# The z sums of a linear-attention layer on VectorE, and its FFN weights and transposes placed anew

## The chip, the cores and the metric

The kernel runs on one core of a Trainium2 chip. The core has TensorE (PE, matmuls into PSUM), VectorE (DVE), ScalarE (ACT), GpSimd (POOL) and SyncE (SP), which here only issues DMAs. The metric is the device time of one execution in microseconds. The kernel before takes 817.4 us, the median of 5 runs from 817.06 to 817.52.

## The reference

One transformer block, forward and backward, in bf16: x has 2048 tokens of D = 640, with H = 32 heads of 20, and the FFN is 1728 wide. Only the part in which the change lies is shown.

```python
def _A_ref(x, wqkv, wo):                      # x is layernormed
    ...
    phi = lambda t: jnp.where(t > 0, t + 1, jnp.exp(t)) + 1e-6
    pq, pk = phi(q), phi(k)
    kv = jnp.einsum("bhsd,bhse->bhde", pk, v)
    z = jnp.einsum("bhsd->bhd", pk)
    num = jnp.einsum("bhqd,bhde->bhqe", pq, kv)
    den = jnp.einsum("bhqd,bhd->bhq", pq, z)[..., None] + 1e-6
    o = num / den
    return ... @ wo
h = x + _A_ref(_layernorm(x), A_wqkv, A_wo)
h2 = h + _B_ref(_layernorm(h), ...)           # (silu(x @ w_gate) * (x @ w_up)) @ w_down
```

The kernel gives h2 and the gradients of x and of all weights for a given grad_out. z, one number per column of pk, is the sum of pk over all 2048 tokens.

## The kernel before, in words

Tokens lie in 16 tiles of 128 (partitions), columns in 5 blocks of 128; a row of 640 columns goes through PSUM as two halves of 320. All of PSUM is four buffers of two banks (`mm`, line 63), given out in turn. SBUF has two pools of large buffers, `big` (5 tiles with tag B) and `strips` (4 with tag S); a new tile waits until the last reader of the one whose place it takes has ended, a DMA among them.

The stages around the change, with the times of the profiled execution:

1. **Layernorm, q and k** (lines 324 to 383, until 55 us). `kq_mm` makes k and q of a tile; ACT writes exp and relu of them; `phi` (line 310) makes pk and pqa of that on DVE with two instructions, and every four tiles stores pk, or pq and xnT, on SP. The last calls, for the tiles 12 to 15, are at lines 374 to 376.
2. **Y and z** (lines 478 to 494, 55 to 86 us). Y^T = xn^T pk in five columns of 2 x 16 matmuls (line 482). `z_sum` (line 467) sums pk over the tokens with 32 matmuls against ones of 128 x 32, of which four use different 32-column strips of PE; ACT and DVE split the sum into a bf16 value and a bf16 remainder; four matmuls with 1/32 (line 489) sum the partitions, giving zb, the same in every partition, by which DVE gets the denominators.
3. **Normalise** (`normalise`, line 439, four tiles at a time): product with zb, sum over each head, reciprocal, multiply into pqa, and then `tr_pqs` (line 450), one DMA transpose per tile into pqsT. Groups 0 and 4 come after Y, groups 8 and 12 after W2.
4. **KVT and W2** (lines 501 to 524, 86 to 95 us): small matmuls, masked on DVE, then W2^T with one DMA transpose per block.
5. **The attention loop** (lines 533 to 565, 98 to 146 us). Per tile, ten matmuls (`ps_a`, line 539), the residual added on DVE into the x row `xr`, statistics on DVE, rstd on POOL. Two iterations later the row goes out to `scr_h1` from ACT's queue, `hn` is written on DVE, and SP transposes it into hnT. `load_xr` loads the x rows ahead, into six small buffers.
6. **FFN** (from line 568, 146 us). Four weight groups. pg and pu (lines 593 and 598) need `hnT` and the gate and up weights of the group, `wgu`, loaded by `load_wgu` (line 182) into one of two buffers; group 0 takes that of wdT, which the dm steps of groups 0 and 1 read.

**dm steps** (`dm_steps`, line 399): 24 pieces of ten matmuls of 448 or 384 columns for the backward pass, which need nothing of the attention. They are put between other work by `dm(n)`: nine ahead of the attention loop, one inside its first row and one after each of the rows 1 to 14.

**The order of the work.** Inside `tc.manual_schedule(engines=...)` the named engines issue in the order of the program; the others are ordered by a planner that estimates costs. From line 461 on that is so for PE, DVE and SP, so ACT and POOL are planned. A DMA stands in the queue of the engine that issues it. `tc.keep_in_program_order` fixes one instruction, `tc.issue_after(x)` puts what follows behind x on x's engine.

Of the kernel before, what the change touches and what calls it, by code (L numbers as in the profile page):

```python
# [20 lines left out]
def kernel(  # L21
# [159 lines left out]

    def load_wgu(g):
        w = GW[g]
        t = wpool.tile([P, DT, 2 * GM], BF16, name="wgu", tag="wgu")
        nc.sync.dma_start(out=t[:, :, 0:w], in_=B_w_gate[:, GO[g]:GO[g] + w].rearrange("(k p) n -> p k n", p=P))
        nc.sync.dma_start(out=t[:, :, w:2 * w], in_=B_w_up[:, GO[g]:GO[g] + w].rearrange("(k p) n -> p k n", p=P))
        return t

# [41 lines left out]
    with tc.manual_schedule(engines={EngineType.Pool}):  # L230
# [6 lines left out]
        E = const.tile([P, D], BF16, name="E")  # L237
    ones32 = const.tile([P, P], BF16, name="ones32")
    nc.vector.memset(ones32[:], 1.0 / H)
    zpad = const.tile([P, 4, 64], BF16, name="zpad")  # L240
# [69 lines left out]
    def phi(which, t, n=2):  # L310
        e = (pk, pqa)[which][:, t:t + n, :]
        nc.vector.tensor_scalar(out=e, in0=e, scalar1=1.0, scalar2=1e-6, op0=ALU.min, op1=ALU.add)
        nc.vector.tensor_tensor(out=e, in0=e, in1=rr[:, 2 * which + t // 2 % 2, t % 2:t % 2 + n, :], op=ALU.add)
        if (t + n) % 4 == 0:
            sl = slice(t + n - 4, t + n)
            if which == 0:
                nc.sync.dma_start(out=scr_pk_v[:, sl, :], in_=pk[:, sl, :])
            else:
                nc.sync.dma_start(out=scr_pq_v[:, sl, :], in_=pqa[:, sl, :])
                nc.sync.dma_start(out=scr_xnT[sl].rearrange("t p k c -> p t k c"), in_=xnT[:, sl])  # L320

    PIECES = ((0, 3), (3, DT))

    with tc.manual_schedule(engines={EngineType.PE, EngineType.DVE, EngineType.Activation, EngineType.Pool}):
# [33 lines left out]
        for t in range(2, ST):  # L358
            if t == 2:
                ln1_stats(4)  # L360
            if t > 3 and t + 3 < ST:
                ln1_stats(t + 3)
            kq_mm(t, 0, (lambda: copy1(t + 1)) if t + 1 < ST else None)
            if t == 2:
                ln1_stats(5)
            if t == 3:
                ln1_stats(6)
            if t == ST - 1:
                phi(0, t - 1, 1)
            kq_mm(t, 1)  # L370
            if t == 3:
                phi(1, 0)
            elif t == ST - 1:
                phi(0, t, 1)
                phi(1, t - 3)
                phi(1, t - 1)
            elif t > 3:
                phi(t % 2, t - 2 - t % 2)
            if t + 2 < ST:
                ln1_xn(t + 2)  # L380
            if ST - NC - 1 <= t < ST - 1:
                ln1_xn(t - ST + NC + 1)

    fA.close()
    fpool = wB.enter_context(tc.tile_pool(name="fpool", bufs=6))

# [32 lines left out]
    def masks():  # L421
        tc.keep_in_program_order(nc.gpsimd.memset(mask[:], 1.0))
        for c0, n, p0 in ((0, 6, 0), (120, 2, 88)):
            m = mask[:, c0:c0 + n * Dh]
            for sign in (1, -1):
                tc.keep_in_program_order(nc.gpsimd.affine_select(
                    out=m, in_=m, pattern=[[-sign * Dh, n], [0, Dh]], compare_op=ALU.is_ge, fill=0.0,
                    base=-p0 if sign > 0 else p0 + Dh - 1, channel_multiplier=sign))

# [6 lines left out]
    def hb4(ap):  # L436
        return ap.rearrange("p t (h e) -> p t h e", e=Dh)

    def normalise(t):

        pq = pqa[:, t:t + 4, :]
        tz = tzs[:, t % 8:t % 8 + 4, :]
        nc.vector.tensor_tensor(out=tz, in0=pq, in1=zb[:].unsqueeze(1).to_broadcast([P, 4, D]), op=ALU.mult)
        den = small.tile([P, 4, H], FP32, name="den", tag="den", bufs=2)
        nc.vector.tensor_reduce(out=den[:], in_=hb4(tz), axis=AX.X, op=ALU.add)
        nc.vector.tensor_scalar(out=den[:], in0=den[:], scalar1=1e-6, scalar2=None, op0=ALU.add)
        nc.vector.reciprocal(out=rall[:, t:t + 4, :], in_=den[:])
        nc.vector.tensor_tensor(out=hb4(pq), in0=hb4(pq), in1=bc4(rall[:, t:t + 4, :]), op=ALU.mult)

    def tr_pqs(t):  # L450
        for tt in range(t, t + 4):
            nc.sync.dma_start_transpose(out=pqsT[:, :, tt * P:(tt + 1) * P], in_=pqa[:, tt, :])
# [7 lines left out]

    with tc.manual_schedule(engines={EngineType.PE, EngineType.DVE, EngineType.SP}):
        yk = strips.tile([P, DT * D + HG * P], BF16, name="yk", tag="S")
        Yt = yk[:, :DT * D].rearrange("p (k n) -> p k n", k=DT)
        KVT = yk[:, DT * D:].rearrange("p (j c) -> p j c", j=HG)
        zs = [wk("zs"), wk("zl")]

        def z_sum():
            ps = mm("ps_z")
            for ci, (n0, n1) in enumerate(NCH):
                for t in range(ST):  # L470
                    q = t % 4 * H
                    nc.tensor.matmul(ps[q:q + H, ci, :320], lhsT=ones[:, :H], rhs=pk[:, t, n0:n1],
                                     start=(t < 4), stop=(t >= ST - 4))
            nc.scalar.copy(out=half(zs[0][:]), in_=row(ps))
            nc.vector.tensor_tensor(out=half(zs[1][:]), in0=row(ps), in1=half(zs[0][:]), op=ALU.subtract)
            nc.vector.memset(KVT, 0.0)

        for i in range(DT):
            ps = mm("ps_y")
            for ci, (n0, n1) in enumerate(NCH):  # L480
                for t in range(ST):
                    nc.tensor.matmul(ps[:, ci, :320], lhsT=xn[:, t, i * P:(i + 1) * P], rhs=pk[:, t, n0:n1],  # L482
                                     start=(t == 0), stop=(t == ST - 1))
                if (i, ci) == (0, 0):
                    z_sum()
            nc.scalar.copy(out=half(Yt[:, i, :]), in_=row(ps))
            if i == 0:
                ps_z = mm("ps_zb")
                mm_row(ps_z, lambda k: ones32[:], lambda k, n0, n1: zs[k][:, n0:n1], 2)
                nc.scalar.copy(out=half(zb[:]), in_=row(ps_z))  # L490
                masks()
            if 0 < i < 4:
                dm(1)
        dm(1)
        for t in (0, 4):
            normalise(t)
            tr_pqs(t)
        for t in range(6):
# [13 lines left out]

        kv_blocks(KVT, "ps_kvt", lambda i, a, b: wv[:, i, a:b], lambda i, a, b: Yt[:, i, a:b])

        W2T = wv
        W2 = wo6[:, 0:5]
        dm(1)
        for i in range(DT):
            if i % 2 == 0 and i > 0:
                dm(1)  # L520
            ps = mm("ps_w2t")
            mm_heads(ps, lambda j: wo6[:, j, i * P:(i + 1) * P], lambda j, a, b: KVT[:, j, a:b])
            nc.scalar.copy(out=half(W2T[:, i, :]), in_=row(ps))
            nc.sync.dma_start_transpose(out=W2[:, :, i * P:(i + 1) * P], in_=W2T[:, i, :])
        for t in (8, 12):
            normalise(t)
            tr_pqs(t)
        dm(2)

        hn = big.tile([P, ST, D], BF16, name="hn", tag="B")  # L530
        hnT = big.tile([P, DT, S], BF16, name="hnT", tag="B")
        h1s = {}
        for t in range(ST + 2):
            if t < ST:
# [10 lines left out]
                ln_stats(xr[:], mv[:, 0, :])  # L545
                ln_rstd(mv, rstd2, t, 1)
                h1s[t] = (xr, mv)
                if t > 0:
                    dm(1)
            if t > 2:  # L550
                load_xr(t + 3)
            u = t - 2
            if u < 0:
# [5 lines left out]
            if u == 2:  # L559
                nc.sync.dma_start(out=mat_v(scr_W2T), in_=W2T)  # L560
            h1, mv = h1s.pop(u)
            nc.scalar.dma_start(out=scr_h1_v[:, u, :], in_=h1[:])
            nc.vector.tensor_scalar(out=hn[:, u, :], in0=h1[:], scalar1=mv[:, 0, 0:1],
                                    scalar2=rstd2[:, u:u + 1], op0=ALU.subtract, op1=ALU.mult)
            nc.sync.dma_start_transpose(out=hnT[:, :, u * P:(u + 1) * P], in_=hn[:, u, :])


    with tc.manual_schedule(engines={EngineType.SP}):
# [6 lines left out]
        wgT = {}  # L575
        wgu = {0: load_wgu(0)}

# [6 lines left out]
        for g in range(4):  # L584
# [4 lines left out]
            for t in range(0, ST, 2):  # L589
# [25 lines left out]
                if g == 0 and t == 2:  # L615
                    wait_for(sig, load_dh2())
                    wgu[1] = load_wgu(1)
                nc.scalar.activation(out=nsg, in_=pg[:, :, :w], func=ACT.Sigmoid, scale=-1.0)
# [19 lines left out]
            elif g == 1:  # L638
                wgT[0] = big.tile([P, 14, D], BF16, name="wgT", tag="B")
                for gg in range(2):  # L640
                    tr_wgT(gg)
                    wgu[gg + 2] = load_wgu(gg + 2)
            elif g == 2:
# [403 lines left out]
```

## Time and profile before

| | |
|---|---|
| time, median of 5 | 817.4 us |
| time of the profiled execution | 817.73 us |
| its span in the profile | 815.8 us |
| PE busy | 811.5 us, 99% |
| DVE, ACT, POOL busy | 442.4, 288.8, 192.3 us |
| DMA, mean over the span | 194 GB/s |
| TensorE clock granted | 1.0 throughout |

The span runs from the first to the last instruction; the time is a little longer. Lines of the profile that begin with a number and an engine are instructions in order of time: start, duration, engine, line of the kernel, operation, output <- inputs, shape, and how many were merged; in square brackets, how long the engine was idle before it and who ended that. An engine name with a q (SPq) is its queue of issued DMAs.

### The profile page before, as it was taken

How to read it: one execution, taken by the hardware profiler on the slowest of the kernel's cores; microseconds unless marked ns; L12 is line 12 of the kernel's file. 1: busy time of each engine (PE TensorE's matmuls, PEld its weight loads, DVE VectorE, ACT ScalarE, POOL GpSimd, SP SyncE). 2: the span in 40 equal slices, each digit the busy share in tenths (PEclk: the TensorE clock that was granted, in tenths of full speed). 3: DMA queues.
4: the chain of work that ended last, by engine and by line, in shares of the span. 5: the costliest groups of instructions: out<-in, count | busy, mean ns of one | idle time of the engine just before them, and what ended most of it. 6: DMA issues, size and time to landing. Idle time of an engine off the chain costs nothing.

```text
span 815.8 us, 13979 instructions
## 1 busy us (share of the span) xinstructions
PE 811.5 (99%) x5540; PEld 522.7 (64%) x5540; DVE 442.4 (54%) x849; ACT 288.8 (35%) x406; POOL 192.3 (24%) x350
## 2 busy tenths in 40 slices
PE   9999999999999999999999999999999999999998
PEld 7776666555555555555566677777777777777676
DVE  7878787890086028800760147787892366631212
ACT  6982432760184126400841122322322133322010
POOL 3420022212512412221125401211220121112330
PEclk9999999999999999999999999999999999999999
DMA  9994799899769987994498757976498999999972
GB/s 303 188 358 89 166 193 291 174 238 217 201 133 217 221 195 158 212 224 116 115 252 172 262 118 219 223 197 176 113 235 170 169 173 177 166 203 249 207 208 78
DMA packets 278321, 158.61 MB, mean 194 GB/s; under 512 B 235053, under 2 KB 264878, under 8 KB 278257
## 3 DMA queue, kind: packets, MB, share of 16 engines
q1 hardware_dynamic: 251696, 82.12, 54.1%
q0 software_dynamic: 17744, 64.45, 26.1%
q10 hardware_dynamic: 8816, 11.16, 4.4%
q8 instruction: 43, 0.70, 0.4%
q14 instruction: 22, 0.17, 0.1%
HBM read 47.68 MB, written 53.66 MB: 124 GB/s over the span
## 4 chain that ended last, share of the span: by engine, by line
PE 99%; POOL 0%; issue 0%; DVE 0%; POOLq 0%
PE ps_dw L665 21%; PE ps_dhn L109 14%; PE ps_dxn L917 8%; PE ps_o L979 7%; PE pg L593 7%; PE pu L598 7%; PE ps_kq L302 5%; PE ps_dwqk L109 5%; PE ps_dm L396 5%; PE ps_y L482 3%; PE ps_dp L109 3%; PE ps_dk L109 3%; PE ps_gt L724 3%; PE ps_a L539 3%; PE pdm L396 2%; PE ps_warm L330 1%
## 5 line engine op out<-in xcount | busy, mean ns | idle before, releaser
L109 PE MATMUL ps_dhn<-wgT,cols 128*128 128x320 bf16 x864 | 119.5, 299 | 0.0
L665 PE MATMUL ps_dw<-dd,hn 128*128 128x448 bf16 (+1 forms) x640 | 118.8, 346 | 0.0
L109 PEld LDWEIGHTS <-cols 128*128 128x128 bf16 x864 | 84.5, 98 | 32.9
L665 PEld LDWEIGHTS <-hn 128*128 128x128 bf16 x640 | 62.6, 98 | 54.2
L667 DVE CAST dwev<-ps_dw 128x896 bf16<-128x896 f32 (+3 forms) x12 | 10.9, 907 | 123.6 <-PE ps_dw L665 123.6
L667 ACT CAST dwev<-ps_dw 128x896 bf16<-128x896 f32 (+1 forms) x20 | 17.6, 878 | 157.6 <-PE ps_dw L665 150.6
L630 POOL DMA_DIRECT2D scr_dT<-stg x64 | 34.6, 541 | 164.0 <-DMA stg<-dd 160.0
L147 DVE CUSTOM_DVE_ANT_0 lb_a<-lb_dy,hn 128x640 bf16<-128x640 bf16 x32 | 26.4, 826 | 76.1 <-ACT lb_dy L145 76.1
L598 PE MATMUL pu<-wgu,hnT 128*128 128x448 bf16 (+1 forms) x320 | 63.6, 346 | 0.0
L593 PE MATMUL pg<-wgu,hnT 128*128 128x448 bf16 (+1 forms) x320 | 63.6, 346 | 0.0
L979 PE MATMUL ps_o<-wd,mT 128*128 128x320 bf16 (+3 forms) x462 | 61.1, 295 | 0.0
L665 PE MATMUL ps_dw<-m_s,dh 128*128 128x448 bf16 (+1 forms) x320 | 60.4, 346 | 0.0
L917 PEld LDWEIGHTS <-ring 128*128 128x128 bf16 x480 | 47.0, 98 | 18.2
L979 PEld LDWEIGHTS <-mT 128*128 128x128 bf16 (+1 forms) x462 | 41.8, 97 | 17.4 <-issue 2.6
L917 PE MATMUL ps_dxn<-wqkvT,ring 128*128 128x320 bf16 x320 | 51.3, 299 | 0.0
L598 PEld LDWEIGHTS <-hnT 128*128 128x128 bf16 x320 | 31.3, 98 | 27.1
L665 PEld LDWEIGHTS <-dh 128*128 128x128 bf16 x320 | 31.3, 98 | 27.1
L593 PEld LDWEIGHTS <-hnT 128*128 128x128 bf16 x320 | 31.3, 98 | 27.0
L396 PE MATMUL ps_dm<-wdT,dh2T 128*128 128x448 bf16 (+1 forms) x240 | 47.0, 344 | 0.0
L396 PEld LDWEIGHTS <-dh2T 128*128 128x128 bf16 x320 | 31.0, 98 | 24.9
L302 PE MATMUL ps_kq<-wqk,xnT 128*128 128x320 bf16 x320 | 46.5, 300 | 0.0
L145 ACT ACTIVATE lb_dy<-ps_dhn,rstd 128x640 bf16<-128x640 f32 x16 | 12.7, 793 | 88.7 <-PE ps_dhn L109 88.7
(167 smaller groups left out, 1276.8 us busy)
## 6 DMA issues: line engine op xcount, KB each, us to landing
scr_dT<-stg POOLq DMA_DIRECT2D x48, 224.0 KB, 3.4
cols<-scr_dT POOLq DMA_DIRECT2D x6, 1728.0 KB, 7.9
scr_m<-m_s POOLq DMA_DIRECT2D x12, 448.0 KB, 4.6
cols<-scr_dT ACTq DMA_DIRECT2D x2, 1728.0 KB, 9.7
out_dram<-dwev POOLq DMA_DIRECT2D x30, 112.0 KB, 2.7
scr_dT<-stg POOLq DMA_DIRECT2D x16, 192.0 KB, 2.7
scr_pk<-pk SPq DMA_DIRECT2D x4, 640.0 KB, 8.2
scr_xnT<-xnT SPq DMA_DIRECT2D x4, 640.0 KB, 8.2
```

Of the source, the lines that this page charges most:

```text
L109: nc.tensor.matmul(ps[:, ci, :320], lhsT=lhs(k), rhs=rhs(k, *NCH[ci]), start=(start and k == 0), stop=(stop and k == n - 1))
L147: nc.vector.tensor_tensor_reduce(out=a[:], in0=dy[:], in1=xhat, scale=1.0, scalar=0.0, op0=ALU.mult, op1=ALU.add, accum_out=sums[:, 1:2])
L302: nc.tensor.matmul(ps[:, ci, :320], lhsT=xnT[:, t, k, :], rhs=wqk[:, k, w0 + n0:w0 + n1], start=(k == 0), stop=(k == DT - 1))
L396: nc.tensor.matmul(ps[:, c, :w], lhsT=dh2T[:, kt, (t + c) * P:(t + c + 1) * P], rhs=wdT[:, kt, o:o + w], start=(kt == 0), stop=(kt == DT - 1))
L482: nc.tensor.matmul(ps[:, ci, :320], lhsT=xn[:, t, i * P:(i + 1) * P], rhs=pk[:, t, n0:n1], start=(t == 0), stop=(t == ST - 1))
L593: nc.tensor.matmul(pg[:, c, :w], lhsT=hnT[:, kt, (t + c) * P:(t + c + 1) * P], rhs=wg[:, kt, 0:w], start=(kt == 0), stop=(kt == DT - 1))
L598: nc.tensor.matmul(pu[:, c, :w], lhsT=hnT[:, kt, (t + c) * P:(t + c + 1) * P], rhs=wg[:, kt, w:2 * w], start=(kt == 0), stop=(kt == DT - 1))
L630: nc.gpsimd.dma_start(out=scr_dT[t + c, :, KO[g]:KO[g] + GK[g], :], in_=stg[:, :GK[g], :])
L665: nc.tensor.matmul(ps[:, c, :w], lhsT=lhs(t), rhs=rhs(t), start=(t == 0), stop=(t == ST - 1))
L667: last = copy(out=ev[:, :len(parts), :w], in_=ps[:, :len(parts), :w])
L917: nc.tensor.matmul(ps[:, ci, :320], lhsT=lhs[:, i, :], rhs=rhs[:, i, n0:n1], start=(k == 0 and i == 0), stop=(k == 2 and i == DT - 1))
L979: nc.tensor.matmul(po(t, ci), lhsT=mTs[t // 4][r, t % 4, j, :], rhs=wd[r, j, n0:n1], start=(t, ci) not in opened, stop=last)
```

## The change

- z is summed on DVE: seven adds over pairs of token tiles into an fp32 tile of 128 x 1280 (which lies in the second half of the strip `tzs`), one add of its two halves, then the same split into a bf16 value and a remainder. `z_sum` and its 32 matmuls go; the four matmuls that sum the partitions (`z_bcast`) use ones and come after the third column of Y instead of the first.
- The last two phi calls for q (tiles 12 to 15) come behind the z adds on DVE, with their stores on SP. `masks` comes to POOL's fixed order.
- `normalise` is split into `norm_den` and `norm_mul`. The multiply of group 4 comes behind the masking of KVT, its transposes behind those of W2.
- Five dm steps instead of two stand ahead of the attention loop, so twelve in all; rows 3, 7 and 11 of the loop have none.
- The transposes of pqsT 12 to 15 go out one per row in rows 0 to 3 of the loop.
- h1 rows are stored from POOL's queue, one row later, instead of from ACT's, two rows later. POOL has a fixed order in this stage.
- The gate weights of FFN group 0 are loaded in row 7 and the up weights in row 9 of the loop, instead of behind it.
- hnT is allocated in row 3; its transposes start in row 4, one per row, three in row 14.

```diff
-                phi(0, t, 1)
-                phi(1, t - 3)
-                phi(1, t - 1)
+                last_phi = phi(0, t, 1)
...
-    with tc.manual_schedule(engines={EngineType.PE, EngineType.DVE, EngineType.SP}):
+    with tc.manual_schedule(engines={EngineType.PE, EngineType.DVE, EngineType.SP, EngineType.Pool}):
...
+        z2 = tzs[:, 4:8].rearrange("p t d -> p (t d)").bitcast(FP32)
+        zf = z2[:, :D]
+        tok2 = pk.rearrange("p (t two) d -> p t (two d)", two=2)
+        with tc.issue_after(last_phi):
+            nc.vector.tensor_tensor(out=z2, in0=tok2[:, 0], in1=tok2[:, 1], op=ALU.add)
+        for t in range(2, ST // 2):
+            nc.vector.tensor_tensor(out=z2, in0=z2, in1=tok2[:, t], op=ALU.add)
+        nc.vector.tensor_tensor(out=zf, in0=zf, in1=z2[:, D:], op=ALU.add)
         zs = [wk("zs"), wk("zl")]
-        def z_sum():
...
+        nc.vector.tensor_copy(out=zs[0][:], in_=zf)
+        nc.vector.tensor_tensor(out=zs[1][:], in0=zf, in1=zs[0][:], op=ALU.subtract)
+        for t in (ST - 4, ST - 2):
+            phi(1, t)
+        nc.vector.memset(KVT, 0.0)
+        masks()
+        def z_bcast():
+            ps = mm("ps_zb")
+            mm_row(ps, lambda k: ones[:], lambda k, n0, n1: zs[k][:, n0:n1], 2)
+            nc.scalar.copy(out=half(zb[:]), in_=row(ps))
...
-                if (i, ci) == (0, 0):
-                    z_sum()
+                if (i, ci) == (2, 1):
+                    z_bcast()
...
-        for t in (0, 4):
-            normalise(t)
-            tr_pqs(t)
+        norm_den(0)
+        norm_mul(0)
+        tr_pqs(0)
+        norm_den(4)
...
         kv_blocks(KVT, "ps_kvt", lambda i, a, b: wv[:, i, a:b], lambda i, a, b: Yt[:, i, a:b])
+        norm_mul(4)
...
+        tr_pqs(4)
         for t in (8, 12):
-            normalise(t)
-            tr_pqs(t)
-        dm(2)
+            norm_den(t)
+            norm_mul(t)
+            if t < 12:
+                tr_pqs(t)
+        dm(5)
...
-                if t > 0:
+                if t > 0 and t % 4 != 3:
                     dm(1)
+            if t in (7, 9):
+                load_wgu(0, t // 9)
+            while h1_todo and h1_todo[0][0] < t:
+                v, h1 = h1_todo.pop(0)
+                nc.gpsimd.dma_start(out=scr_h1_v[:, v, :], in_=h1[:])
             if t > 2:
                 load_xr(t + 3)
+            if t < 4:
+                tr_pqs(12 + t, 1)
+            if t == 3:
+                hnT = big.tile([P, DT, S], BF16, name="hnT", tag="B")
...
-            nc.scalar.dma_start(out=scr_h1_v[:, u, :], in_=h1[:])
...
-            nc.sync.dma_start_transpose(out=hnT[:, :, u * P:(u + 1) * P], in_=hn[:, u, :])
+            hnT_todo.append(u)
+            for v in hnT_todo[:0 if t < 4 else 1 if t < 14 else 3]:
+                hnT_todo.pop(0)
+                nc.sync.dma_start_transpose(out=hnT[:, :, v * P:(v + 1) * P], in_=hn[:, v, :])
```

The pool `fpool` is also opened behind this stage instead of ahead of it, and `load_wgu` takes an argument for which of the two halves to load.

More of the change, by code (lines that the diff above doesn't have):

```diff
@@ L180, in fw, with load_wgu @@
         return fpool.tile([P, 2, GM], BF16, name=name, tag="f")
-    def load_wgu(g):
+    wgu = {}
+    def load_wgu(g, which=None):
         w = GW[g]
[L184 to L187, printed above, removed]
+        if which != 1:
+            wgu[g] = wpool.tile([P, DT, 2 * GM], BF16, name="wgu", tag="wgu")
+        for k, src in enumerate((B_w_gate, B_w_up)):
+            if which in (None, k):
+                nc.sync.dma_start(out=wgu[g][:, :, k * w:(k + 1) * w],
+                                  in_=src[:, GO[g]:GO[g] + w].rearrange("(k p) n -> p k n", p=P))
     x_tm = [strips.tile([P, 8, D], BF16, name="x_tm", tag="S") for _ in range(2)]
@@ L237 @@
         E = const.tile([P, D], BF16, name="E")
-    ones32 = const.tile([P, P], BF16, name="ones32")
-    nc.vector.memset(ones32[:], 1.0 / H)
     zpad = const.tile([P, 4, 64], BF16, name="zpad")
@@ L312, in phi @@
         nc.vector.tensor_scalar(out=e, in0=e, scalar1=1.0, scalar2=1e-6, op0=ALU.min, op1=ALU.add)
-        nc.vector.tensor_tensor(out=e, in0=e, in1=rr[:, 2 * which + t // 2 % 2, t % 2:t % 2 + n, :], op=ALU.add)
+        last = nc.vector.tensor_tensor(out=e, in0=e, in1=rr[:, 2 * which + t // 2 % 2, t % 2:t % 2 + n, :], op=ALU.add)
         if (t + n) % 4 == 0:
@@ L320, in phi @@
                 nc.sync.dma_start(out=scr_xnT[sl].rearrange("t p k c -> p t k c"), in_=xnT[:, sl])
+        return last.ins
     PIECES = ((0, 3), (3, DT))
@@ L382 @@
                 ln1_xn(t - ST + NC + 1)
-    fA.close()
-    fpool = wB.enter_context(tc.tile_pool(name="fpool", bufs=6))
     dm_t = {0: strips.tile([P, ST, GM], BF16, name="dm0", tag="S")}
@@ L421, in masks @@
     def masks():
-        tc.keep_in_program_order(nc.gpsimd.memset(mask[:], 1.0))
+        nc.gpsimd.memset(mask[:], 1.0)
         for c0, n, p0 in ((0, 6, 0), (120, 2, 88)):
@@ L425, in masks @@
             for sign in (1, -1):
-                tc.keep_in_program_order(nc.gpsimd.affine_select(
+                nc.gpsimd.affine_select(
                     out=m, in_=m, pattern=[[-sign * Dh, n], [0, Dh]], compare_op=ALU.is_ge, fill=0.0,
-                    base=-p0 if sign > 0 else p0 + Dh - 1, channel_multiplier=sign))
+                    base=-p0 if sign > 0 else p0 + Dh - 1, channel_multiplier=sign)
     pqsT = big.tile([P, DT, S], BF16, name="pqsT", tag="B")
@@ L437, in hb4, with norm_den @@
         return ap.rearrange("p t (h e) -> p t h e", e=Dh)
-    def normalise(t):
+    def norm_den(t):
         pq = pqa[:, t:t + 4, :]
@@ L447, in normalise, with norm_mul, tr_pqs @@
         nc.vector.reciprocal(out=rall[:, t:t + 4, :], in_=den[:])
+    def norm_mul(t):
+        pq = pqa[:, t:t + 4, :]
         nc.vector.tensor_tensor(out=hb4(pq), in0=hb4(pq), in1=bc4(rall[:, t:t + 4, :]), op=ALU.mult)
-    def tr_pqs(t):
-        for tt in range(t, t + 4):
+    def tr_pqs(t, n=4):
+        for tt in range(t, t + n):
             nc.sync.dma_start_transpose(out=pqsT[:, :, tt * P:(tt + 1) * P], in_=pqa[:, tt, :])
@@ L464 @@
         KVT = yk[:, DT * D:].rearrange("p (j c) -> p j c", j=HG)
-        zs = [wk("zs"), wk("zl")]
-        def z_sum():
[L468 to L476, printed above, removed]
+        z2 = tzs[:, 4:8].rearrange("p t d -> p (t d)").bitcast(FP32)
[6 more added lines that the diff above has]
+        nc.vector.tensor_tensor(out=zf, in0=zf, in1=z2[:, D:], op=ALU.add)
+        zs = [wk("zs"), wk("zl")]
+        nc.vector.tensor_copy(out=zs[0][:], in_=zf)
[8 more added lines that the diff above has]
+            nc.scalar.copy(out=half(zb[:]), in_=row(ps))
         for i in range(DT):
@@ L483 @@
                                      start=(t == 0), stop=(t == ST - 1))
-                if (i, ci) == (0, 0):
-                    z_sum()
+                if (i, ci) == (2, 1):
+                    z_bcast()
             nc.scalar.copy(out=half(Yt[:, i, :]), in_=row(ps))
[L487 to L491, printed above, removed]
             if 0 < i < 4:
@@ L524 @@
             nc.sync.dma_start_transpose(out=W2[:, :, i * P:(i + 1) * P], in_=W2T[:, i, :])
+        tr_pqs(4)
         for t in (8, 12):
-            normalise(t)
-            tr_pqs(t)
-        dm(2)
+            norm_den(t)
[3 more added lines that the diff above has]
+        dm(5)
         hn = big.tile([P, ST, D], BF16, name="hn", tag="B")
-        hnT = big.tile([P, DT, S], BF16, name="hnT", tag="B")
         h1s = {}
+        h1_todo = []
+        hnT_todo = []
         for t in range(ST + 2):
@@ L546 @@
                 ln_rstd(mv, rstd2, t, 1)
+                h1_todo.append((t, xr))
                 h1s[t] = (xr, mv)
-                if t > 0:
+                if t > 0 and t % 4 != 3:
                     dm(1)
+            if t in (7, 9):
[3 more added lines that the diff above has]
+                nc.gpsimd.dma_start(out=scr_h1_v[:, v, :], in_=h1[:])
             if t > 2:
                 load_xr(t + 3)
+            if t < 4:
+                tr_pqs(12 + t, 1)
+            if t == 3:
+                hnT = big.tile([P, DT, S], BF16, name="hnT", tag="B")
             u = t - 2
@@ L561 @@
             h1, mv = h1s.pop(u)
-            nc.scalar.dma_start(out=scr_h1_v[:, u, :], in_=h1[:])
             nc.vector.tensor_scalar(out=hn[:, u, :], in0=h1[:], scalar1=mv[:, 0, 0:1],
                                     scalar2=rstd2[:, u:u + 1], op0=ALU.subtract, op1=ALU.mult)
-            nc.sync.dma_start_transpose(out=hnT[:, :, u * P:(u + 1) * P], in_=hn[:, u, :])
+            hnT_todo.append(u)
+            for v in hnT_todo[:0 if t < 4 else 1 if t < 14 else 3]:
+                hnT_todo.pop(0)
+                nc.sync.dma_start_transpose(out=hnT[:, :, v * P:(v + 1) * P], in_=hn[:, v, :])
+    fA.close()
+    fpool = wB.enter_context(tc.tile_pool(name="fpool", bufs=6))
     with tc.manual_schedule(engines={EngineType.SP}):
@@ L575 @@
         wgT = {}
-        wgu = {0: load_wgu(0)}
         def tr_wgT(g):
@@ L616 @@
                     wait_for(sig, load_dh2())
-                    wgu[1] = load_wgu(1)
+                    load_wgu(1)
                 nc.scalar.activation(out=nsg, in_=pg[:, :, :w], func=ACT.Sigmoid, scale=-1.0)
@@ L641 @@
                     tr_wgT(gg)
-                    wgu[gg + 2] = load_wgu(gg + 2)
+                    load_wgu(gg + 2)
             elif g == 2:
```

## The prediction

> **What bounds the kernel now.** First the busy line of the page, then the stretches around the change, then the order of time on PE.
>
> ```profile
> PE 811.5 (99%) x5540; PEld 522.7 (64%) x5540; DVE 442.4 (54%) x849; ACT 288.8 (35%) x406; POOL 192.3 (24%) x350
> ...
> PE 99%; POOL 0%; issue 0%; DVE 0%; POOLq 0%
> ```
>
> Busy time and chain agree: PE. The next view tells whether that holds where the change is (columns: stretch; PE, PEld, DVE, ACT, POOL busy with instructions; clock; DMA share; GB/s).
>
> ```profile
> 55.00:98.00 43.00, 43.00 (x351) 28.14 (x349) 31.72 (x29) 16.40 (x23) 0.00 (x0) 1.00 0.64 161
> 98.00:146.00 48.00, 48.00 (x310) 30.21 (x309) 39.08 (x77) 15.04 (x18) 12.32 (x29) 1.00 0.98 232
> 146.00:454.00 308.00, 308.00 (x1689) 165.00 (x1687) 142.26 (x243) 120.28 (x149) 88.20 (x155) 1.00 0.84 191
> ```
>
> PE has no gap at full clock: from 8 to 813 us it lacks 0.11 us of 805. So a step gains only what it takes off PE, and costs only what it makes PE wait. No removed DVE, ACT or DMA time counts by itself. The reader also sees that DMA is full (0.98) in the attention loop and not before it (0.64).
>
> **What leaves PE.** The 32 z matmuls, in order of time on PE:
>
> ```profile
> 54.84 2.34 PE L482 MATMUL ps_y<-pk,xn 128*128 128x320 bf16 x16
> 57.10 1.27 PE L472 MATMUL ps_z<-pk,ones 128*32 128x320 bf16 x32
> 58.31 2.35 PE L482 MATMUL ps_y<-pk,xn 128*128 128x320 bf16 x16
> ...
> 61.03 4.51 PE L482 MATMUL ps_y<-pk,xn 128*128 128x320 bf16 x32
> ```
>
> A column of Y (32 matmuls) starts every 4.35 us in the chain of waits. The two halves of the first column and the z block between them run from 54.84 to 60.49, 5.65 us; 5.65 - 4.35 = 1.30 us is what z costs, with the small gaps where the 128x32 tiles begin and end. The four ps_zb matmuls (60.49 to 61.03, 0.54 us) stay, only later; with weights 1.0 for 1/32, since the 32 copies of each sum are gone. The 24 dm steps are all still there: 3 + 1 + 1 + 2 + 5 = 12 ahead of the loop, one in t = 0, eleven in t = 1, 2, 4, 5, 6, 8, 9, 10, 12, 13, 14. PE's sum is -1.30 us.
>
> **What z costs VectorE, and when PE wants it.** Rows of DVE:
>
> ```profile
> 55.28 0.49 DVE L313 TENSOR_TENSOR pk<-pk,rr 128x640 bf16<-128x640 bf16 x1 [0.27 <-ACT rr L308]
> 55.69 0.49 DVE L312 TENSOR_SCALAR pqa<-pqa 128x1280 bf16<-128x1280 bf16 x1
> 56.21 0.83 DVE L313 TENSOR_TENSOR pqa<-pqa,rr 128x1280 bf16<-128x1280 bf16 x1
> ...
> 59.15 0.82 DVE L475 TENSOR_TENSOR zl<-ps_z,zs 128x640 bf16<-128x640 f32 x1 [0.79 <-ACT zs L474]
> 60.00 0.38 DVE L476 MEMSET yk<- 128x384 uint32 x1
> ...
> 63.54 2.82 DVE L445 TENSOR_REDUCE den<-tzs 128x128 f32<-128x2560 bf16 x1
> ```
>
> The trace has no fp32 add from SBUF. The nearest rows: bf16 pairs, 1280 elements in 0.83 (the cheap end), and one element at a time, 640 in 0.82 with an f32 operand and 2560 in 2.82. The last two lie on one line, 0.157 us plus 1.04 ns per element, which gives 1.49 for 1280; the dear end is the whole 2.82. I take 1.49, because a stream with an f32 operand is what the 0.82 row is, and 1.52 with the 0.03 between dependent instructions. Seven adds from 55.80: 66.47. Folding the halves 0.82, the bf16 copy 0.49, the remainder 0.82, each plus 0.03: z is ready at 68.7. PE comes to ps_zb, after three columns and one dm step, at 54.84 + 3 x 4.35 + 1.89 = 69.78. Slack about 1.0 us after the hand-over. [...]
>
> Behind z wait, in DVE's queue: two pqa phi pairs (0.49 + 0.83 each), the memset (0.38), then normalisation. So their scr_pq and scr_xnT stores on SP go from 58 to about 72 us; SP had nothing else to issue between 58.8 and 70.5, and xnT's buffer, which pqsT may take, is free (stores of 640 KB landed in 8 us at a full DMA) by 80. The first den group (1.49 + 2.82 + 0.23 + 0.95 + gaps) runs 71.7 to 77.3, its multiply to 80.1, the second den group to 85.8. There the second multiply is split off, so the KVT masking is not behind it: ps_kvt ends on PE at 86.1, the masking at 87.1, and PE wants it at 89.32 - 1.30 = 88.0. Slack again 1.0 us. Then multiply 4 to 89.9, groups 8 and 12 to 106.8. Attention begins on PE at 98.37 + 3 x 1.89 - 1.30 = 102.7, its first row is complete at 106.0, and DVE takes it at 106.8, less behind than now (row complete at 101.6, taken at 104.66). The three added dm steps are the cover for the 12 us of adds.
>
> **The attention loop.** A row with its dm step takes PE 3.25 (later 2.99), without one 1.36; four rows take 11.1, later 10.3. DVE needs about 2.3 per row with hn (0.82 + 0.92 + 0.13 + 0.40), 9.2 per four. It keeps up. ACT loses 16 store issues (0.33 each); POOL gains them at 0.54 to 0.76 (its rows for such issues), beside 0.9 of rstd per row: 1.6 of 2.6 us. Behind a store on POOL stands only the next rstd, wanted two rows later. [...]
>
> SP is the queue to watch. Its rows for the window 45 to 160 us (min/median/max ns, first and last start), for the transposes
>
> ```profile
> L452 SPq DMA_TRANSPOSE pqsT<-pqa x16: 1201/1276/2909, 70.5 to 110.3; - x16
> ```
>
> and for the x rows, with their landing:
>
> ```profile
> L459 SPq DMA_DIRECT2D xr<-in_A_x_dram x16: 333/552/1572, 84.1 to 138.9; - x16
> ...
> DMA to landing us min/median/max: 2.4/3.4/6.6
> ```
>
> In the new order, at 1.3 per transpose: pqsT 0 to 3 from 80.1, x rows and scr_Yt to 88.6, five W2 transposes to about 97.5 (as W2T comes), pqsT 4 to 7 to 102.8, 8 to 11 to 108, 12 to 15 one per row to 115, hnT one per row from about 118 (its buffer is pqa's, free when pqsT 15 has landed). W2 is wanted at 102.7, pqsT 4 at 113.8, 8 at 124.4, 12 at 134.7: all early. x row 8 would issue at 119.5, wanted at 127, and lands in 6.6 at the worst. A late row stops PE only when the fourth PSUM tile after it is asked for, some 3.4 us later. The weight halves go out near 124 and 129.5 (now 123.4 and 126.2); 10.9 us was the slowest landing of such a piece, so 140.4, against pu at 147.0. hnT 10 to 12 leave at t = 14, their first use is at 164. Nothing is added.
>
> **Sum.** 817.73 (the profiled execution; its span is 815.8 and 1.93 lies around it) - 1.30 = 816.43. That execution is 0.33 above the median 817.4, so the forecast is **816.1**. A difference under 0.2% (1.63 us) is about what a measurement here cannot tell from no change; -1.30 is 0.16%, so the likeliest case counts as "within".
>
> **Rivals.**
> 1. *z or KVT is late on VectorE.* PE waits at ps_zb for what exceeds 1.0 us: adds that follow each other at 1.66 use up the slack, at 1.85 the gain; if z were queued behind the two phi pairs (that is, the change did not get the order it writes), PE waits 2.6 - 1.0 = 1.6: 817.7. At the dear end, 2.82 per add, the wait is 7 x 1.33 - 1.0 = 8.3: 824.4. [...] For a small wait: two places with 1.0 us.
> 2. *The loop's DMA does not keep up (slower).* The old loop moved 4.6 + 13.4 + 28.9 = 46.9 us of work for all engines (shares 0.66, 0.96, 1.07 of the stretches 98 to 105, 105 to 119, 119 to 146). The new loop lasts 42.4 us with the same transposes, x rows, stores and weights: a share of 1.11. If the 4.5 us excess falls on the x rows and PE waits for all of it: 820.6. It decides from a wait of 2.9 us (1.30 + 1.63). For it: DVE already waited 1.1 us for one x row at 135. Against it: the 5 us stretches from 130 to 140 reached 1.17 and 1.13 without a gap on PE, and PSUM and the early x rows take up about 4 us first. A part of it, under 2.1 us, gives up to 818.2.
> 3. *More comes free.* I find nothing: PE's starts from 54.84 to 146.43 add up to its matmuls within 0.1 us.
>
> **How the numbers follow.** Forecast 0.60, of which 0.10 lies under 815.8 (815.6 at the lowest, an unseen half of a microsecond). z late by a little 0.09, at the dear end 0.05. Loop wait under 2.9 us 0.14, above 0.12. So faster 0.10, within 0.50 + 0.09 + 0.14 = 0.73, slower 0.17. The range runs from 815.6 to 818.2 and leaves out the two dear ends and the dearer part of a loop wait, 0.2.
>
> **What would show it.** Right: no ps_z; adds of 1.49; ps_zb beginning about 69.8 with no idle before it; attention from 102.7; the first pg at 146.43 - 1.30 = 145.1; PE without gaps. Wrong by 1: idle on PE before ps_zb or ps_w2t, released by DVE. Wrong by 2: xr add waiting for DMA for over 3 us, and ps_a or ps_dm waiting for DVE. Wrong altogether: a gap on PE after 146, where I changed nothing.

## The result

The changed kernel takes 815.91 us, the median of 26 runs, against 817.52 of 44 runs of the kernel before. The ratio is 0.9981, 95% interval 0.9976 to 0.9987: 1.6 us less, with an interval from 1.1 to 2.0. Forecast were 1.3 less, 816.1. The profiled execution took 815.81 us, its span 814.1. Of the 1.6 us, 1.4 lie in the span (medians 815.6 and 814.2) and 0.2 outside it: what an execution takes beyond its span is 1.85 to 1.98 us in the runs of all five kernels here that store the h1 rows from ACT, the kernel before among them, and 1.66 to 1.77 in the runs of all nine that store them from POOL; `h1_act` below differs from the changed kernel in that alone. The page's busy line and chain of the changed kernel:

```profile
PE 809.6 (99%) x5508; PEld 521.5 (64%) x5508; DVE 453.2 (56%) x857; ACT 288.2 (35%) x405; POOL 201.3 (25%) x366
...
PE 99%; POOL 0%; ACT 0%; issue 0%; DVE 0%; POOLq 0%
```

PE has 32 matmuls fewer, DVE is busy 10.8 us longer, and the chain is still PE from end to end. The stretches around the change (same columns as before, each stretch begun or ended 1 us earlier with the work):

```profile
55.00:97.00 42.00, 42.00 (x319) 27.57 (x317) 40.84 (x35) 15.50 (x22) 0.00 (x0) 1.00 0.53 142
97.00:145.00 48.00, 48.00 (x311) 30.33 (x310) 40.35 (x77) 15.13 (x18) 19.91 (x41) 1.00 0.94 226
145.00:453.00 308.00, 308.00 (x1688) 165.07 (x1687) 142.90 (x246) 120.86 (x148) 89.81 (x157) 1.00 0.82 194
```

PE has no gap in any of them. DVE went from 31.7 of 43 to 40.8 of 42 us in the first: it is nearly full there, which is why the experiments below look at what it would do if it were a little later. On PE, in order of time:

```profile
54.62 8.86 PE L491 MATMUL ps_y<-pk,xn 128*128 128x320 bf16 x64
63.31 2.06 PE L394 MATMUL ps_dm<-wdT,dh2T 128*128 128x448 bf16 x10
65.20 4.51 PE L491 MATMUL ps_y<-pk,xn 128*128 128x320 bf16 x32
69.55 0.30 PE L109 MATMUL ps_zb<-zs,ones 128*128 128x320 bf16 x1
```

The first two columns of Y now follow each other, and ps_zb begins with no idle time in brackets. From the first Y matmul to the first pg it was 146.43 - 54.84 = 91.59 us and is 144.81 - 54.62 = 90.19: 1.40 us less, where the prediction had 1.30. The z block is 1.31 of it: to the dm step behind the second column it was 65.38 - 54.84 = 10.54 us, of which ps_zb was 0.54, and is 63.31 - 54.62 = 8.69. The other 0.09 lies in the attention loop, and `rest_only` below, with z on PE, has it too. From pg to the end of the span the two differ by 0.1. The rest of the 1.7 between the two spans is the start of Y, 0.2 earlier; over the fourteen kernels profiled here it lies between 54.36 and 54.99 whatever stands behind it, so it is scatter.

On DVE:

```profile
55.46 1.48 DVE L470 TENSOR_TENSOR tzs<-pk 128x1280 f32<-128x1280 bf16 x1
56.98 9.12 DVE L472 TENSOR_TENSOR tzs<-tzs,pk 128x1280 f32<-128x1280 f32 x6
66.14 0.83 DVE L473 TENSOR_TENSOR tzs<-tzs 128x640 f32<-128x640 f32 x1
67.00 0.49 DVE L475 CAST zs<-tzs 128x640 bf16<-128x640 f32 x1
67.53 0.83 DVE L476 TENSOR_TENSOR zl<-tzs,zs 128x640 bf16<-128x640 f32 x1
```

An fp32 add of 1280 takes 1.48, six in a row 1.52 each: about 1 ns per element (0.65 us for the 640 by which the first and the folding add differ), whether the inputs are bf16 or f32, as the line through the old rows said. z is ready at 68.36, PE wants it at 69.55: 1.2 us of slack.

### The profile page after: what moved, and what is told of

It is laid out like the page before. It is cut to its first block, busy times and chain, and to the rows that moved or that the text cites. A ratio compares the mean times of both kernels' runs of the same rounds, so it can differ in the third digit from the quotient of the medians.

```text
span 814.1 us, 13916 instructions
## 1 busy us (share of the span) xinstructions
PE 809.6 (99%) x5508; PEld 521.5 (64%) x5508; DVE 453.2 (56%) x857; ACT 288.2 (35%) x405; POOL 201.3 (25%) x366
## 4 chain that ended last, share of the span: by engine, by line
PE 99%; POOL 0%; ACT 0%; issue 0%; DVE 0%; POOLq 0%
PE ps_dw L689 22%; PE ps_dhn L109 14%; PE ps_dxn L941 8%; PE ps_o L1003 7%; PE pg L617 7%; PE pu L622 7%; PE ps_kq L304 5%; PE ps_dwqk L109 5%; PE ps_dm L394 5%; PE ps_gt L748 3%; PE ps_dk L109 3%; PE ps_dp L109 3%; PE ps_y L491 3%; PE ps_a L549 3%; PE pdm L394 2%; PE ps_warm L333 1%
```

## What was tried

My theory was that the 1.3 to 1.4 us are the z block and nothing else, and that the other parts only hide the work that z puts on DVE. The rival was that the new places of the dm steps, transposes and stores gain by themselves. After that came the question which of the other parts is needed. All times are medians; the kernel before, run beside them on the same chips, was 817.5 to 817.6.

**Each half alone.** `rest_only` is the changed kernel with z on PE again:

```diff
-        (z2, the adds, the late phi calls, z_bcast after the third column)
+                phi(1, t - 3)
+                phi(1, t - 1)
...
+                if (i, ci) == (0, 0):
+                    z_sum()
```

> The changed kernel with z back on PE as before (32 matmuls in the first column, the phi pairs at their old place), everything else of the change kept. Theory: the z block is back, 1.30 to 1.40 us, and PE has no gap: 817.2 to 817.5. Rival (the new placement of dm steps, transposes and stores is what gains): 816.0.

Measured: 817.35, ratio 1.0001 (0.9992 to 1.0010), and PE waits nowhere behind the start. On PE the new placement gains 0.09 us by itself (91.50 from the first Y matmul to pg, against 91.59), and the 0.2 outside the span come with it: 817.35 against 817.53, which the interval does not tell from nothing. The theory holds for the 1.3 us, and the rival keeps 0.3 at most.

`z_only` is the kernel before with z on DVE as in the change and nothing else:

```diff
+        nc.vector.tensor_tensor(out=z2, in0=z2, in1=tok2[:, t], op=ALU.add)
...
         for t in (0, 4):
             normalise(t)
             tr_pqs(t)
...
         dm(2)
```

> The kernel before with z summed on VectorE alone (the seven adds, the late pq phi pairs, ps_zb after the third column of Y); normalise, dm steps, transposes, stores and weight loads stay as before. Theory (PE is the bound, z's 1.30 us is all the gain, the other parts are cover): group 4 is normalised whole before the KVT masking, which then ends at about 71.3 + 2 x 8.37 + 1.4 = 89.4 where PE wants its last block at about 88.0, so PE waits about 1.4 us before ps_w2t and nothing else: 817.3 to 817.6, no gain over 817.5, with a gap on PE released by DVE. Rival (the gain comes from the transposes, stores and loads being placed anew, and z is worth nothing): 817.5 too, but without a gap on PE. Rival (VectorE's 12 us more reach the attention loop and PSUM runs out): 819 or more, with gaps at ps_a.

Measured: 826.95, ratio 1.0113 (1.0099 to 1.0126), 9.4 us slower than before. The third case had the size (819 or more) and the place (ps_a), but not the reason: it is not PSUM that runs out. The waits of PE (total, times, longest):

```profile
PE ps_a L538 <- DMA wvo<-wvo: 5.0, 1, 5.0
PE ps_dm L391 <- DVE yk L509: 2.2, 1, 2.2
```

The second I had, at 1.4 and one step later. The first I had not: W2 (wvo) came late. Its transposes stand on SP behind pqsT 4 to 7, and those wait for DVE's multiply of group 4:

```profile
80.12 13.48 SPq L447 DMA_TRANSPOSE pqsT<-pqa  x8
93.64 5.23 SPq L454 DMA_DIRECT2D xr<-in_A_x_dram  x6
98.96 0.40 SPq L499 DMA_DIRECT2D scr_Yt<-yk  x1
99.45 8.49 SPq L523 DMA_TRANSPOSE wvo<-wvo  x5
```

W2's transposes begin at 99.45, in the changed kernel at 89.51. The late engine is DVE, but what PE meets is a queue in which a transfer that nobody needs yet stands ahead of one that PE needs. And behind both gaps the granted clock fell (the third number from the end):

```profile
88.60:92.00 3.40, 3.35 (x10) 1.40 (x10) 3.37 (x5) 0.00 (x0) 0.00 (x0) 0.56 0.50 96
...
106.40:110.50 4.10, 4.07 (x16) 1.99 (x17) 0.00 (x0) 0.00 (x0) 0.00 (x0) 0.62 0.67 120
```

Ten dm matmuls take 3.36 us there instead of 1.89. By PE's starts the two gaps cost 2.4 and 5.2 us, and the slow matmuls 1.5 + 0.2 behind the first and 0.6 + 0.9 behind the second, 3.2 in all. That is 10.7 (with rounding) of the 11.1 us by which its span exceeds that of the changed kernel; the other 0.4 is its later start of Y.

**How much slack z has.** `add1` and `add3` are the changed kernel with one and three more adds ahead of the folding add:

```diff
+        zx = tzs[:, 0:4].rearrange("p t d -> p (t d)").bitcast(FP32)
+        for t in range(3):
+            nc.vector.tensor_tensor(out=zx, in0=z2, in1=tok2[:, t], op=ALU.add)
         nc.vector.tensor_tensor(out=zf, in0=zf, in1=z2[:, D:], op=ALU.add)
```

> The changed kernel with one more fp32 add of 128 x 1280 on VectorE ahead of the folding add (into a part of the strip that nothing reads). z was ready at 68.36 and wanted at 69.55 in the profile of the changed kernel; the add takes 1.52. Theory: PE waits 0.3 to 0.5 us before ps_zb: 816.2 to 816.5. Rival (the slack is larger than the profile shows, or the dm steps behind take the delay up): 815.9.

> The same with three more adds, 4.56 us. Theory: PE waits 4.56 - 1.2 = 3.4 us before ps_zb and nowhere else, since all that follows moves with it: 819.2 to 819.5, slower than before by 0.2%. Rival (the twelve dm steps are cover for it, the wait is made up later): 816 to 817.

Measured: `add1` 817.03, ratio 0.9995 (0.9986 to 1.0003), 1.1 above the changed kernel; `add3` 821.48, ratio 1.0042 (1.0030 to 1.0055), 5.6 above it. Both lose more than expected. ps_zb does what it should: by PE's starts 0.25 are lost there in `add1`, and in `add3` 3.3, these two lines with the idle time in brackets:

```profile
72.25 0.31 PE L109 MATMUL ps_zb<-zs,ones 128*128 128x320 bf16 x1 [2.42 <-DVE zs L478]
73.10 0.30 PE L109 MATMUL ps_zb<-zl,ones 128*128 128x320 bf16 x1 [0.54 <-DVE zl L479]
```

But in `add1` PE waits again at the KVT step:

```profile
86.80 0.28 PE L515 MATMUL ps_kvt<-yk,wvo 128*128 128x40 bf16 x5 [0.70 <-DVE yk L518]
```

This is the fourth ps_kvt tile, and what it waits for is a PSUM buffer: DVE begins the masking at 86.52 and has the first tile masked at 86.74. In the changed kernel it began at 85.09 and had it at 85.31, and the fourth tile started at 85.77. By starts `add1` loses 0.86 here, and 0.25 + 0.86 is its 1.1. `add3` loses 0.7 at this place too, at the dm step behind the tile, and 1.5 more at 181 us, where ps_dw waits for a load of dh: POOL issued it at 171.82, behind two scr_dT stores that waited for their transposes, and at 164.42 in the changed kernel. A delay on DVE can so be paid for again 100 us later, in a queue.

`add1_rec` tests the reading of the PSUM buffer:

```diff
         den4 = norm_den(4)
...
         kv_blocks(KVT, "ps_kvt", ...)
+        norm_rec(4, den4)          # the 1e-6 and the reciprocal
         norm_mul(4)
```

> The kernel add1 (one more fp32 add) with the last two small instructions of group 4's denominators (the 1e-6 and the reciprocal, 0.23 + 0.95) moved behind the KVT masking. In add1 PE waited 0.7 us for the fourth tile of ps_kvt, whose PSUM buffer came free only when VectorE had masked the first. Theory (that buffer, and not the masking's end, is what PE meets first): the masking begins 1.2 us earlier, the wait at ps_kvt is gone, and only about 0.3 us at ps_zb are left: 816.2 to 816.4 against 817.0 for add1. Rival (the time of add1 comes from elsewhere, as VectorE's lateness in the attention loop): 817.0.

Measured: 816.44, ratio 0.9983 (0.9974 to 0.9991); the wait at ps_kvt is gone and 0.25 at ps_zb is left, as much as pg comes later than in the changed kernel (0.26 from the first Y matmul). The buffer it was.

**Which part of the cover is needed.** `unsplit` has group 4 normalised whole ahead of the masking:

```diff
         norm_den(4)
+        norm_mul(4)
...
         kv_blocks(KVT, "ps_kvt", ...)
-        norm_mul(4)
```

> The changed kernel with group 4 normalised whole ahead of the KVT masking; its transposes stay behind those of W2, all else as changed. The masking then begins at 85.1 + 2.8 = 87.9; the fourth tile of ps_kvt wants a PSUM buffer at 85.8 and gets one at 88.2. Theory: PE waits 2.4 us at ps_kvt: 818.3, up to 820 if the granted clock drops behind it as in z_only (gap 2.2 us, clock 0.56 for 3.4 us). Rival (only the order on SP cost z_only its time): 816.0 to 816.5.

Measured: 818.32, ratio 1.0015 (1.0007 to 1.0023), with one gap and the clock at 1.0:

```profile
88.36 2.05 PE L394 MATMUL ps_dm<-wdT,dh2T 128*128 128x448 bf16 x10 [2.22 <-DVE yk L516]
```

As the theory said, one PSUM tile later than I put it: the fourth ps_kvt tile found a buffer, the dm step behind it did not. The four buffers are thus not given out strictly in turn. In `add1` and the changed kernel the fourth tile takes the first masked one's place and the dm step that of the dm step before; here and in `add3` it is the other way round.

`dm2` has two dm steps ahead of the loop and one in every row:

```diff
-        dm(5)
+        dm(2)
...
-                if t > 0 and t % 4 != 3:
+                if t > 0:
                     dm(1)
```

> The changed kernel with two dm steps ahead of the attention loop instead of five and one in every row of it, as before. PE then comes to ps_a 5.67 us earlier (96.8), its first row is complete at 100.3, and VectorE takes it at 106.0 as now; three rows and one dm step then hold all four PSUM buffers, and the next row wants one at 106.8, when the first is free. Theory (the five steps are cover for VectorE, and just enough): PE waits 0.3 to 2.5 us at ps_a or ps_dm, or at the first row for the W2 transposes (0.5): 816.5 to 818.5, more if the granted clock drops behind the gap, as it did in z_only. Rival (the steps need not stand there): 816.0 with no gap.

Measured: 816.62, ratio 0.9988 (0.9979 to 0.9996), with an idle time of 0.34 us at ps_dm released by the x-row add (by starts 0.50 there and 0.15 a row earlier). The three steps are worth 0.7 us: with two, DVE is behind by a little more than PSUM can hold.

`core` is `z_only` with the split and with the transposes of group 4 behind those of W2; `old_loop` is `core` with five dm steps ahead and rows 3, 7 and 11 without one:

```diff
         norm_den(4)
...
+        norm_mul(4)                # behind kv_blocks
...
+        tr_pqs(4)                  # behind the transposes of W2
         for t in (8, 12):
```

> The kernel before with three things alone: z on VectorE, the multiply of group 4 behind the KVT masking, and its transposes behind those of W2; two dm steps ahead of the loop, one in every row, the loop as before. It differs from z_only by the split and the order of SP. Theory (these two took z_only's 9.4 us: 2.2 at the KVT masking, 5.0 for W2 transposes that stood behind those of pqsT 4 to 7 on SP, and the clock that dropped behind both): 816 to 818, no gap at ps_kvt, at most 2 us at the first rows of ps_a. Rival (the five steps or the loop's new order are what is needed): 820 or more.

> The changed kernel with its attention loop as before: pqsT 12 to 15 transposed ahead of the loop, hnT transposed as soon as a row of hn is there, weights of FFN group 0 placed by the planner, h1 rows stored from ACT two rows later, POOL planned. z on VectorE, the split multiply of group 4, its transposes behind those of W2, and the five dm steps stay. Theory (the new placement in the loop is worth nothing by itself, since x rows are early by some us): 815.8 to 816.3, no gap on PE. Rival (the loop's DMA does not keep up without it): x rows late, gaps at ps_a or ps_dm, 817 to 820.

Measured: `core` 820.75, ratio 1.0041 (1.0024 to 1.0057); `old_loop` 820.54, ratio 1.0033 (1.0023 to 1.0043). The split and SP's order take away `z_only`'s two gaps. But the attention loop as it was before no longer works behind them: new gaps stand there, and five dm steps do not help. Both theories fell: `core` came out where its rival stood, and the loop's new order is worth much. In `old_loop` ACT's rows

```profile
127.25 0.41 ACTq L407 DMA_DIRECT2D scr_dm<-dmst  x1
127.77 5.31 ACTq L568 DMA_DIRECT2D scr_h<-xr  x2
133.13 0.80 ACT L405 CAST dmst<-ps_dm 128x768 bf16<-128x768 f32 x1 [8.34 <-DMA scr_h<-xr]
```

stand ahead of PE's

```profile
133.98 3.36 PE L391 MATMUL ps_dm<-wdT,dh2T 128*128 128x384 bf16 x10 [2.46 <-ACT dmst L405]
```

The planner put two h1 stores (rows 7 and 8) in a row ahead of a copy that frees PSUM; the second store goes out five microseconds after the first, the copy behind it, and PE stands for 2.46 and then runs at a clock of 0.78 (mean of 135 to 140 us). DVE waited 2.5 us for an x row in the same stretch. So two causes are left, ACT's queue and late x rows. Three kernels part them:

```diff
# h1_act: the changed kernel with
-                nc.gpsimd.dma_start(out=scr_h1_v[:, v, :], in_=h1[:])
+                nc.scalar.dma_start(out=scr_h1_v[:, v, :], in_=h1[:])
# old_pool: old_loop with
-            nc.scalar.dma_start(out=scr_h1_v[:, u, :], in_=h1[:])
+                nc.gpsimd.dma_start(out=scr_h1_v[:, v, :], in_=h1[:])
# hnT_asap: the changed kernel with
-            for v in hnT_todo[:0 if t < 4 else 1 if t < 14 else 3]:
+            for v in hnT_todo[:0 if t < 3 else 3]:
```

> The changed kernel with its h1 stores issued from ACT's queue, one row later as in the changed kernel; nothing else differs. In old_loop PE waited 2.5 us for a dmst copy that stood in ACT's queue behind two h1 stores. Theory (ACT's queue is what failed in old_loop: a store that must wait holds the copies that free PSUM): a gap on PE at ps_dm released by ACT, 816.5 to 820. Rival (the stores on ACT are harmless as long as the x rows and transposes are placed as now): 815.9, no gap.

> old_loop with its h1 stores issued from POOL in program order, one row later, as in the changed kernel; the transposes of pqsT 12 to 15 and hnT and the FFN weights stay placed as in old_loop. Theory (ACT's queue is what failed): no gap at ps_dm, 815.8 to 816.5, though x rows come late as in old_loop (2.5 us on VectorE), since four PSUM buffers take that. Rival (the transfers crowd the DMA engines and the x rows come too late for PE): 818 to 820, gaps released by VectorE.

> The changed kernel with hnT transposed as soon as its row of hn is written (from row 3 on), so that SP waits for VectorE in every row; all else as changed. Theory (the lag of the hnT transposes is not what keeps PE busy): 815.8 to 816.2, no gap. Rival (SP, waiting for hn, sends the x rows late): x rows awaited on VectorE for over 2 us, 816.5 to 819.

Measured: `h1_act` 817.09 (815.99 to 820.12), ratio 0.9992 (0.9983 to 1.0001); `old_pool` 818.94, ratio 1.0007 (0.9996 to 1.0018); `hnT_asap` 818.60, ratio 1.0007 (0.9998 to 1.0016). `h1_act` was profiled in an execution of 820.12, the longest of its 11: it has one gap of 2.24 us at ps_dm behind a copy on ACT, as in `old_loop`, so ACT's queue does hold PE, though not in every execution: the fastest (815.99) has the changed kernel's span, 814.1. The copy behind the second store names a load of gate weights that it has no use for:

```profile
132.99 0.80 ACT L408 CAST dmst<-ps_dm 128x768 bf16<-128x768 f32 x1 [7.08 <-DMA wgu<-in_B_w_gate_dram]
```

What the store waited for, the trace shows. In the traces a DMA that lands steps up a semaphore (a counter): 10224 steps for 639 DMAs, 16 each, in the kernel before and in the changed one. The instruction on ACT just ahead of this store waits for the semaphore that the store itself will raise. The last DMA on it was that gate load, issued by SP at 125.82 and landed at 132.54; the store goes out at 132.62, though its row (8) was ready on DVE at 127.34. In `old_loop` it is the same row's store: ready at 128.76, issued at 132.76, behind the load of x row 9 by SP, issued at 127.29 and landed at 132.66, the same landing for which DVE waited 2.5 us. In all fourteen traces the DMAs of SP and ACT share eight semaphores and those of POOL have eight others; in each trace 623 DMAs follow another on their semaphore, and every one is issued after that one has landed. So a store on ACT can stand behind a slow load of SP, and the copy that frees PSUM behind the store; a store on POOL has no load of SP ahead of it.

`old_pool` has no gap behind ACT and 1.5 us behind DVE. `hnT_asap` differs from the changed kernel in the order of transposes alone; DVE's wait for x rows in its loop and the widest gap on PE are

```profile
DVE xr L553 <- DMA xr<-in_A_x_dram: 7.3, 4, 2.8
```

```profile
137.74 1.79 PE L394 MATMUL ps_dm<-wdT,dh2T 128*128 128x384 bf16 x10 [1.45 <-DVE xr L553]
```

SP's rows around x row 7 are these, in `hnT_asap` first and then in the changed kernel:

```profile
118.09 2.56 SPq L587 DMA_TRANSPOSE hnT<-hn  x2
120.71 0.58 SPq L460 DMA_DIRECT2D xr<-in_A_x_dram  x1
```

```profile
116.93 0.34 SPq L460 DMA_DIRECT2D xr<-in_A_x_dram  x1
```

The row goes out 3.8 us later, behind two transposes, the first of which waits 1.7 us for the place of hnT. The next transpose, at 121.83, takes 2.36 us where others take 1.2 to 1.5, since hn is late, and the loads of rows 8 to 11 stay 3.5 to 4.1 us behind those of the changed kernel. So the lag of the hnT transposes is worth 2.7 us, more than the whole gain: without it the change would be no faster than the kernel before. That is my second rival, which I had given 0.26, in the one place where the change provides against it. My expectations for `hnT_asap` and `old_pool` failed, as those for `core` and `old_loop` had.

## Why the prediction was right

- *PE is the bound, and the z block is the gain.* Right: 1.31 for 1.30, and `rest_only` gives it back. The sum took the 1.93 us around the span as fixed and the loop as worth nothing by itself; 0.2 and 0.09 came from there, and with them 1.6 was measured for 1.3. Why stores from ACT lengthen what lies outside the span stays open.
- *Adds of 1.49, z at 68.7, slack 1.0.* Right: 1.48 and 1.52 in a row (the dear end was 2.82), 68.36, 1.2. `add1` and `add3` show that PE waits there for what exceeds it.
- *KVT is wanted at 88.0, slack again 1.0.* The size of the slack was wrong, without effect on the time. I asked when the masked result is wanted; what PE wants first is the PSUM buffer of an unmasked tile, two steps earlier. By `add1`, where DVE was 1.43 later, PE 0.16 later and the loss by starts 0.86, the slack is about 0.4.
- *Attention from 102.7, first pg at 145.1.* 102.51 and 144.81, with the 0.2 earlier start.
- *The stores cost POOL 0.54 to 0.76 and hold only the next rstd.* 0.63 each at the median and 0.80 at most, but SP holds for them: the load of an x row needs the place of a stored one, and SP waited 6.9 us in all for h1 stores to land (median 4.4 us; from ACT 3.7 before and 3.3 in `h1_act`). One x row did come late. DVE's row is

```profile
139.06 0.82 DVE L553 TENSOR_TENSOR xr<-ps_a,xr 128x640 bf16<-128x640 f32 x1 [2.06 <-PE ps_a L549]
```

  and names PE, but PE had that tile ready:

```profile
133.14 2.88 PE L549 MATMUL ps_a<-wvo,pqsT 128*128 128x320 bf16 x20
```

  These are rows 11 and 12, complete at 136. The load of row 12 went out on SP at 134.17, after 3.1 us of waiting for an h1 store, and landed at 138.94: it was the x row. PSUM took the 2 us up.
- *Rival 2, the loop's DMA.* Its share of 0.12 and 0.14 was not too much: PSUM had to take up 2 us in the changed loop, and `old_pool`, `hnT_asap` and `old_loop` went over. My arithmetic (46.9 us of transfers in 42.4, a share of 1.11) was too high for the loop as a whole: from 102.5 to 144.8 the share is 1.00, and eight hnT transposes go out from 140.6 on, in part behind it. In single stretches of 5 us from 110 to 145 it is 0.89 to 1.25. What decides is which transfer SP issues first (2.7 us in `hnT_asap`), and that I had not weighed: that the order of the change was good enough was luck as far as the prediction goes.

## What to carry to other kernels

Where one engine has no gaps, a change gains what it takes off that engine, to a tenth of a microsecond on that engine here (1.40 us for 1.30 predicted), and the work moved elsewhere has to be paid for in places: follow the loaded engine's later start to every buffer that it frees and to every in-order queue that waits for it, not only to its results. A transfer that waits for the late engine must not stand ahead of one that the bound engine needs; moving it behind was worth more (5.0 us, and 1.5 us more at the granted clock of 0.62 behind it) than the whole gain. A part of a change that gains nothing alone may be what lets another gain: here the whole is 1.6 us faster, z alone is 9.4 slower, the rest alone the same within the interval.

## What the chip showed that was not expected

In some executions the granted clock fell behind a gap on PE. Gaps of 2.22 (`z_only`), 2.46 (`old_loop`) and 2.24 us (`h1_act`) were followed by slow matmuls: the ten dm matmuls right behind them took 3.36, 3.15 and 2.51 us by PE's starts instead of 1.89, 1.63 and 1.63. Gaps of 2.22 (`unsplit`) and 2.42 us (`add3`) were not, in the executions that were profiled. It differs between executions of one kernel, too: three of the twelve of `unsplit` and three of the five of `add3` have a mean granted clock of 0.998 (0.002 of 816 us is 1.6), as the profiled ones of `old_loop` and `h1_act` have, which show one fall each; the others have 1.0. Those three of `unsplit` take 819.9 to 820.3 where its median is 818.3, but one with 1.0 takes 820.8. Why gaps of one length differ, no run here shows. In the three falls behind gaps of 2.2 to 2.5 us the slow matmuls lost 1.7, 1.6 and 1.7 us by PE's starts, and behind the gap of 5.0 us in `z_only` 1.5. So my estimate is that a wait on PE of 2.2 us or more can cost some 1.6 us beyond itself here; whoever prices one should add that as a possibility.
